# Computing the softmax bias of 256 attention blocks on ScalarE in place of GpSimd

## The chip, the cores and the metric

The program runs on one core of one Trainium2 chip. The metric is the device time of one execution in microseconds. Five engines work beside each other, each through its own queue in order: PE (TensorE), DVE (VectorE), ACT (ScalarE), POOL (GpSimd) and SP (SyncE, which here only issues DMAs).

## The reference

Two independent layers are computed and laid side by side in one output of 2048 rows and 2048 columns: attention with a sliding window, and a Fourier mixing layer written as matrix products.

```python
# A: S = 2048, D = 1024, 32 heads of 32, window W = 256
qkv = (x @ wqkv) ...                       # q, k, v
scores = jnp.einsum("bhqd,bhkd->bhqk", q, k) * (Dh ** -0.5)
mask = (idx[:, None] - idx[None, :] >= 0) & (idx[:, None] - idx[None, :] < W)
scores = jnp.where(mask[None, None], scores, -1e9)
o = jnp.einsum("bhqk,bhkd->bhqd", softmax(scores), v)
a = o.reshape(B, S, D) @ wo
# B
a_ = x @ dft_hid_re.T ;  b_ = x @ dft_hid_im.T
b = dft_seq_re @ a_ - dft_seq_im @ b_
out = concatenate([a, b], axis=-1)
```

## The kernel before

**Number format.** Every large product is made of fp16 matmuls: each operand is scaled by a power of two and split into a high part (ACT: a scaled copy to fp16) and a low part (DVE: the same value minus the high part), and three passes, high by high, high by low and low by high, are summed in PSUM (L720).

**Seven products in place of eight.** Most products run by `seven()`: of two by two blocks of each operand, sums are formed first and seven block products are made of them. Between two of these seven, ACT copies a PSUM bank into another (L1193), ACT or DVE evict finished banks (L1509, L1512, L1281, L1284, L431), and PE goes on in the next bank. There are four such banks, `m0` to `m3`.

**Stages.** First q, k and v of the attention are computed (up to some 600 us). Then the Fourier layer runs as a list of units: four rounds, each of eight "x" units (the product along the hidden dimension; results are split and summed into `tsum`, tile name `reg`, L432/L436/L1075) and eight "c" units (the product along the sequence; each loads two tiles of 128 rows of `in_cs`, looks at their largest value on ACT, L1001, scales and splits them on ACT and DVE, L1101 and L1102, and forms four sums on POOL, L1075). A place at which the x units of a round end and its c units begin is called a **turn** below; there are four. Last comes the product with `wo`.

**Attention runs inside these stages.** 256 blocks (8 groups of heads, 4 chunks of 512 rows, 2 pairs of heads, 4 blocks of 128 rows) are fed in between the large products by a counter of matmuls. One block is, in order: scores of two heads (PE, L586), the oldest key block folded in under the mask (DVE, L597), the negative largest score of each row (DVE, `mx`, L602), the softmax **bias** (L606 or L609), two exponentials, one for each head (ACT, L612), the high part (ACT, `hl`, L432), the low part (DVE, L436), one transposing DMA (SP, L621), two masks for the parts outside the window (POOL, `z` L627 and `t` L630). The product with v (PE, L662) follows four blocks later (`LAG`).

The step in question takes a tile of 128 x 2, multiplies it by a scale held per partition and adds a constant:

```python
            if BIAS == "ACT":
                op("ACT", 0.387, lambda: nc.scalar.activation(bias.t, mx.t, AF.Identity, bias=pshift, scale=es),
                   r=[mx, "pshift", ("esc", g // 2)], w=[bias])
            else:
                op("POOL", 0.28, lambda: nc.gpsimd.tensor_scalar(bias.t, mx.t, es, PSHIFT, op0=ALU.mult, op1=ALU.add),
                   r=[mx, ("esc", g // 2)], w=[bias], port=True)
```

**What sets the order.** The operations are not written in the order in which they run. `op()` records each with its engine, a cost in microseconds and what it reads and writes; `Plan.close` works a due time back from the matmuls; `Plan.run` then plays the program through with these costs and gives each free engine the ready operation that is due first. The resulting order is fixed in the program for all engines: a queue never overtakes. So a change of one operation's engine or cost can move any instruction after it. `port=True` marks operations of DVE and POOL that the plan keeps from running at the same time.

Of the kernel before, what the change touches and what calls it, by code (L numbers as in the profile page):

```python
# [46 lines left out]
STP = 4  # L47
RAWS = 6
TBUF = 6
BIAS = "POOL"  # L50
SUMS = ("POOL", "POOL", "POOL", "POOL")
XSUM = "DVE"
PLAIN = 3
# [46 lines left out]
class Plan:  # L100
# [4 lines left out]
    def op(self, eng, cost, fn, r=(), w=(), dma=None, port=False, loose=False):  # L105
        o = Op()
        o.eng, o.cost, o.fn, o.dma, o.port, o.loose = eng, cost, fn, dma, port, loose
        o.pre, o.suc, o.first, o.n, o.aim = set(), [], [], len(self.ops), None
        for k in (*r, *w):
            b = k[0] if isinstance(k, tuple) else k  # L110
            if isinstance(b, Buf) and (not b.ops or b.ops[-1] is not o):
                b.ops.append(o)
        for k in r:
            s = self.state.setdefault(k, [[], []])
            o.pre.update(s[0])
            s[1].append(o)
        for k in w:
            s = self.state.setdefault(k, [[], []])
            o.pre.update(s[0])
            o.pre.update(s[1])  # L120
            self.state[k] = [[o], []]
        o.pre.discard(o)
        self.ops.append(o)
        return o
# [209 lines left out]
def fused_kernel(ctx: ExitStack, tc: tile.TileContext, xa, wqk, wv, wo, xb, wd, cs, out):  # L334
# [194 lines left out]
    def attention():  # L529
# [33 lines left out]
        def s_step(b):  # L563
# [40 lines left out]
            es = escs[:, g // 2, sc:sc + 1]  # L604
            if BIAS == "ACT":
                op("ACT", 0.387, lambda: nc.scalar.activation(bias.t, mx.t, AF.Identity, bias=pshift, scale=es),  # L606
# [1088 lines left out]
```

## Time and profile before

| what | value |
|---|---|
| median of 3 runs | 1726.13 us (1724.79 to 1728.37) |
| the profiled execution | 1728.84 us |
| its span, first to last instruction | 1727.1 us |
| mean granted TensorE clock | 0.998 of full speed |
| DMA queue of SP | 363 MB, 81.6% of 16 engines' span |

The page of the profile lists busy times and the costliest groups of instructions; a group's line names the source line, the engine, the operation, output and inputs, its count, then busy time and mean duration, and after the second bar how long the engine stood idle just before and what ended that. The timeline lists single instructions with start and length, and the idle time of the engine before it in brackets. The windows list the busy time of each engine in a stretch of time.

### The profile page before, as it was taken

How to read it: one execution, taken by the hardware profiler on the slowest of the kernel's cores; microseconds unless marked ns; L12 is line 12 of the kernel's file. 1: busy time of each engine (PE TensorE's matmuls, PEld its weight loads, DVE VectorE, ACT ScalarE, POOL GpSimd, SP SyncE). 2: the span in 40 equal slices, each digit the busy share in tenths (PEclk: the TensorE clock that was granted, in tenths of full speed). 3: DMA queues.
4: the chain of work that ended last, by engine and by line, in shares of the span. 5: the costliest groups of instructions: out<-in, count | busy, mean ns of one | idle time of the engine just before them, and what ended most of it. 6: DMA issues, size and time to landing. Idle time of an engine off the chain costs nothing.

```text
span 1727.1 us, 31901 instructions
## 1 busy us (share of the span) xinstructions
PE 1690.3 (98%) x11607; PEld 908.6 (53%) x11607; DVE 1358.8 (79%) x2294; ACT 1051.5 (61%) x1678; POOL 771.6 (45%) x979
## 2 busy tenths in 40 slices
PE   8999999999999999999999999999999999999998
PEld 3446687675555445555544555545555545544443
DVE  6978997677988888777897986899985679879641
ACT  7555635456757788776675665776665576543322
POOL 0133501224535565635755755676664667611000
PEclk9999999999999999999999999999999999999999
DMA  6388799999998789998599998779999669983331
GB/s 266 121 329 326 229 309 272 267 244 244 221 278 204 159 200 246 215 273 194 98 233 274 246 278 175 151 153 255 238 261 224 141 129 207 215 264 110 110 98 74
DMA packets 469918, 368.36 MB, mean 213 GB/s; under 512 B 341760, under 2 KB 412416, under 8 KB 469760
## 3 DMA queue, kind: packets, MB, share of 16 engines
q1 hardware_dynamic: 468896, 363.17, 81.6%
q0 software_dynamic: 864, 3.15, 1.2%
q8 instruction: 91, 1.49, 0.4%
q14 instruction: 67, 0.55, 0.1%
HBM read 195.97 MB, written 96.86 MB: 170 GB/s over the span
## 4 chain that ended last, share of the span: by engine, by line
PE 83%; DVE 6%; ACT 4%; DMA 3%; issue 3%; POOL 1%; SPq 0%; POOLq 0%; DVEq 0%; ACTq 0%
PE m L720 74%; PE pv L662 4%; PE s L586 3%; PE old L586 1%; DVE st L1102 1%; DMA raw<-in_cs_dram 1%; DVE reg L439 1%; ACT junk L1001 1%; PE m L1323 1%; ACT s L612 1%; ACT reg L432 0%; DVE top L457 0%; DVE mx L602 0%; DVE s L597 0%; DMA late<-in_wo_dram 0%
## 5 line engine op out<-in xcount | busy, mean ns | idle before, releaser
L720 PE MATMUL m<-reg,st 128*128 128x512 f16 x4776 | 1101.1, 379 | 17.5 <-DVE st L1102 3.8
L720 PEld LDWEIGHTS <-st 128*128 128x128 f16 x5400 | 512.4, 98 | 579.1 <-issue 22.0
L612 ACT ACTIVATE s<-s,bias,escs 128x256 f32<-128x256 f32 (+1 forms) x512 | 270.5, 529 | 225.3 <-POOL bias L609 216.3
L609 POOL TENSOR_SCALAR bias<-mx,escs 128x2 f32<-128x2 f32 x256 | 114.2, 446 | 392.2 <-DVE mx L602 334.8
L1075 POOL TENSOR_TENSOR raw<-raw,raw 128x512 f32<-128x512 f32 x128 | 177.4, 1386 | 202.2 <-DVE st L1102 179.8
L436 DVE TENSOR_TENSOR hl<-s,hl 128x512 f16<-128x512 f32 (+1 forms) x256 | 170.6, 668 | 67.6 <-ACT hl L432 64.9
L627 POOL TENSOR_SCALAR_AFFINE_SELECT z<-t 128x512 f16<-128x512 f16 x224 | 174.2, 782 | 53.8 <-DMA t<-hl 41.3
L602 DVE TENSOR_REDUCE mx<-s 128x2 f32<-128x512 f32 (+1 forms) x256 | 170.8, 668 | 4.9
L630 POOL TENSOR_SCALAR_AFFINE_SELECT t<-t 128x512 f16<-128x512 f16 x224 | 169.5, 765 | 9.9
L432 ACT ACTIVATE hl<-s 128x512 f16<-128x512 f32 (+1 forms) x256 | 147.8, 578 | 8.2 <-DMA t<-hl 5.0
L720 PEld LDWEIGHTS <-reg 128*128 128x128 f16 x1212 | 116.3, 98 | 67.2 <-issue 5.2
L1101 ACT ACTIVATE st<-raw,sc 128x1024 f16<-128x1024 f32 x96 | 109.6, 1145 | 59.4 <-PE m L720 30.0
L1102 DVE SCALAR_TENSOR_TENSOR st<-raw,sc,st 128x1024 f16<-128x1024 f32 x96 | 135.8, 1418 | 11.9 <-ACT st L1101 10.7
L586 PEld LDWEIGHTS <-qk 96*128 96x128 f16 x1056 | 93.9, 98 | 81.5 <-issue 8.3
L597 DVE COPY_PREDICATED s<-upper,old 128x256 f32<-128x256 uint32 x224 | 94.6, 422 | 46.6 <-PE old L586 27.2
L720 PE MATMUL m<-reg 128*128 128x512 f16 x480 | 116.3, 382 | 3.5 <-ACT ybig L1509 3.0
L1512 DVE SCALAR_TENSOR_TENSOR ybig<-m,fu,ybig 128x512 f32<-128x512 f32 x112 | 83.4, 745 | 25.4 <-PE m L720 20.9
L720 PE MATMUL m<-xz,st 128*128 128x512 f16 x432 | 97.3, 379 | 2.7 <-ACT m L1193 2.5
L662 PE MATMUL pv<-vt,t 128*128 128x65 f16 x1984 | 98.3, 185 | 0.2
L586 PE MATMUL s<-qk,qk 96*128 96x128 f16 (+1 forms) x608 | 96.1, 253 | 2.0 <-DVE hl L436 1.5
L662 PEld LDWEIGHTS <-t 128*128 128x128 f16 x1984 | 88.3, 96 | 10.8 <-POOL t L630 0.4
L1001 ACT ACTIVATE junk<-raw 128x1024 uint8<-128x1024 f32 x82 | 86.3, 1052 | 10.2 <-DMA raw<-in_cs_dram 9.9
(172 smaller groups left out, 2130.9 us busy)
## 6 DMA issues: line engine op xcount, KB each, us to landing
raw<-in_cs_dram SPq DMA_DIRECT2D x64, 512.0 KB, 5.7
qk<-qs SPq DMA_DIRECT2D x192, 128.0 KB, 3.8
out_dram<-ybig SPq DMA_DIRECT2D x44, 512.0 KB, 4.9
qs<-ybig SPq DMA_DIRECT2D x64, 256.0 KB, 4.5
raw<-in_xb_dram SPq DMA_DIRECT2D x32, 512.0 KB, 5.3
raw<-in_wd_dram SPq DMA_DIRECT2D x32, 512.0 KB, 5.9
ybig<-out_dram SPq DMA_DIRECT2D x32, 512.0 KB, 4.9
vs<-ybig SPq DMA_DIRECT2D x32, 260.0 KB, 4.7
```

What stands on the lines that cost most here:

```text
L432: else nc.scalar.activation(dst(), src(), AF.Copy), r=r, w=w)
L436: op("DVE", c_dve(n), lambda: nc.vector.tensor_tensor(dst(), src(), hi(), op=ALU.subtract), r=r, w=w, port=port)
L586: nc.tensor.matmul(dst(j, a, e), qu.t[:, h, i * P:i * P + P], ku.t[:, h, ka:ke], start=True, stop=True, skip_group_check=True)
L602: dve(c_dve(2 * w), lambda: nc.vector.tensor_reduce(mx.t, sv(), axis=AX.X, op=ALU.max, negate=True), r=[(S, 0), (S, 1)], w=[mx])
L609: op("POOL", 0.28, lambda: nc.gpsimd.tensor_scalar(bias.t, mx.t, es, PSHIFT, op0=ALU.mult, op1=ALU.add), r=[mx, ("esc", g // 2)], w=[bias] ...
L612: op("ACT", 0.32 + 0.00085 * w, lambda h=h: nc.scalar.activation(sv()[:, h], sv()[:, h], AF.Exp, bias=bias.t[:, h:h + 1], scale=es), r=[bi ...
L627: op("POOL", 0.637, lambda: nc.gpsimd.affine_select(out=z.t, in_=pk(), compare_op=ALU.is_gt, fill=0.0, base=0, pattern=[[0, 4], [-1, P]], ...
L630: op("POOL", 0.637, lambda: nc.gpsimd.affine_select(out=pk(), in_=pk(), compare_op=ALU.is_ge, fill=0.0, base=0, pattern=[[0, 4], [1, P]], ...
L662: nc.tensor.matmul(pvt()[:, r, j, lo:], lhs, vt.t[:, k % QB, at + lo:at + VW], start=a, stop=e, skip_group_check=True)
L720: nc.tensor.matmul(ps.t[:, j * n:j * n + n], lhs(), rhs(), start=first, stop=last, skip_group_check=True)
L1075: lambda: e.tensor_tensor(o(), a(), b(), op=ALU.subtract if sub else ALU.add), r=r, w=w, port=True)
L1102: op("DVE", c_dve(n, True), lambda: nc.vector.scalar_tensor_tensor(dst(1), src(), scl(), dst(0), op0=ALU.mult, op1=ALU.subtract), r=[*r, s ...
```

## The change

One constant that chooses the branch above is set to the other value:

```diff
-BIAS = "POOL"
+BIAS = "ACT"
```

The 256 instructions at L609 on POOL go; 256 instructions at L606 on ACT come: an activation with the function Identity, a scale and a bias held per partition. The plan's cost of the step goes from 0.28 to 0.387 us, and the step is no longer marked as using the port that DVE and POOL share. From the first attention block on, the plan sorts the program anew. Of the 256 new instructions, 155 have the first exponential of their block straight behind them.

Early attention blocks on ACT: `s` is the tile of scores, `hl` the split exponentials, `m` a PSUM bank, `kf` a scale.

```order
 L431 ACTIVATE ybig<-m_16_2532,vf 128x16x32
+L606 ACTIVATE bias_3006<-mx_2998,pshift,escs 128x2
 L612 ACTIVATE s_2977<-s_2977,bias_3006,escs 128x256 x2
 L1281 ACTIVATE reg_81<-m_17_2848 128x512
 L432 ACTIVATE hl_3038<-s_2977 128x512
-L612 ACTIVATE s_3020<-s_3020,bias_3041,escs 128x256 x2
+L606 ACTIVATE bias_3042<-mx_3031,pshift,escs 128x2
+L612 ACTIVATE s_3020<-s_3020,bias_3042,escs 128x256 x2
 L431 ACTIVATE ybig<-reg_81,kf 128x512
```

The bias stands in front of its exponentials; the copies and evictions of `m` that follow stand behind both.

The first turn on POOL, before: the four sums (L1075) of one pair of `in_cs` tiles, `raw`, and the biases of three blocks.

```order
L609 TENSOR_SCALAR bias_7175<-mx_7168,escs 128x2
L1075 TENSOR_TENSOR raw_6931<-raw_6931,raw_5477 128x512
L1075 TENSOR_TENSOR raw_5477<-raw_5477 128x512
L609 TENSOR_SCALAR bias_7300<-mx_7271,escs 128x2
L1075 TENSOR_TENSOR raw_5477<-raw_5477,raw_6931 128x512
L609 TENSOR_SCALAR bias_7319<-mx_7311,escs 128x2
```

On ACT, before, the exponentials that need `bias_7300` stand in front of the bank copy L1193:

```order
L1101 ACTIVATE reg_81<-raw_5477,sc_7181 128x512
L612 ACTIVATE s_7195<-s_7195,bias_7300,escs 128x256 x2
L1193 ACTIVATE m_30_7316<-m_36_7260 128x512
L432 ACTIVATE hl_7321<-s_7195 128x512
L1101 ACTIVATE st_7329<-raw_5477,sc_7181 128x1024
```

After the change POOL's four sums stand together, and on ACT the same bank copy (`m_30`) stands behind the split `st_7289` of a summed `raw` and in front of the next bias:

```order
L612 ACTIVATE s_7175<-s_7175,bias_7250,escs 128x256 x2
L432 ACTIVATE hl_7280<-s_7175 128x512
L1101 ACTIVATE st_7286<-raw_6148,sc_7248 128x1024
L1101 ACTIVATE st_7289<-raw_5314,sc_7169 128x1024
L1193 ACTIVATE m_30_7299<-m_36_7234 128x512
L1101 ACTIVATE reg_81<-raw_6318,sc_7248 128x512
L1101 ACTIVATE st_7309<-raw_6923,sc_7169 128x1024
L606 ACTIVATE bias_7320<-mx_7294,pshift,escs 128x2
```

So the copy no longer stands behind exponentials that wait for POOL's bias, but behind a split that waits for POOL's sums.

The fourth turn on SP's queue, before: two `in_cs` loads, and six loads of q and k for the attention (`qk`).

```order
L621 DMA_TRANSPOSE t_18026<-hl_18011 128x8x128
L417 DMA raw_18041<-in_cs_dram 128x1024
L417 DMA qk_39_18050<-qs 32x4x512 x3
L417 DMA qk_31_18063<-qs 32x4x512 x2
L417 DMA raw_18072<-in_cs_dram 128x1024
L417 DMA qk_31_18063<-qs 32x4x512
```

and after:

```order
L621 DMA_TRANSPOSE t_17963<-hl_17911 128x8x128
L417 DMA raw_18011<-in_cs_dram 128x1024
L417 DMA raw_18027<-in_cs_dram 128x1024
L621 DMA_TRANSPOSE t_18039<-hl_18020 128x8x128
L417 DMA qk_39_18054<-qs 32x4x512 x3
L417 DMA qk_31_18066<-qs 32x4x512 x3
```

The second of the two loads stood behind five loads of q and k; now it stands straight behind the first.

The same turn on ACT, before: the looks (L1001, `junk`) at these two tiles and the evictions (L1509) of three banks. The look at the other tile of the pair, `raw_18041`, comes further down.

```order
L1001 ACTIVATE junk,top_18133<-raw_18072 128x1024
L1509 ACTIVATE ybig<-m_65_18081,fu_17758 128x512
L612 ACTIVATE s_18030<-s_18030,bias_18140,escs 128x256 x2
L1509 ACTIVATE ybig<-m_64_18076,fu_17758 128x512
L432 ACTIVATE hl_18167<-s_18030 128x512
```

and after:

```order
L1001 ACTIVATE junk,top_18098<-raw_18011 128x1024
L606 ACTIVATE bias_18113<-mx_18094,pshift,escs 128x2
L1001 ACTIVATE junk,top_18098<-raw_18027 128x1024
L612 ACTIVATE s_18043<-s_18043,bias_18113,escs 128x256 x2
L432 ACTIVATE hl_18132<-s_18043 128x512
L1509 ACTIVATE ybig<-m_64_18079,fu_17760 128x512
L1509 ACTIVATE ybig<-m_83_18048,fu_17760 128x512
```

Both looks now stand ahead of the evictions, and the eviction of bank `m_64` is the first of them. From the `wo` loads near the end on, SP's queue holds the same rows in the same order before and after.

## The prediction

> **What bounds the kernel now.** I read the page first: busy times, then the groups that the change touches.
>
> ```profile
> PE 1690.3 (98%) x11607; PEld 908.6 (53%) x11607; DVE 1358.8 (79%) x2294; ACT 1051.5 (61%) x1678; POOL 771.6 (45%) x979
> ...
> L612 ACT ACTIVATE s<-s,bias,escs 128x256 f32<-128x256 f32 (+1 forms) x512 | 270.5, 529 | 225.3 <-POOL bias L609 216.3
> L609 POOL TENSOR_SCALAR bias<-mx,escs 128x2 f32<-128x2 f32 x256 | 114.2, 446 | 392.2 <-DVE mx L602 334.8
> ```
>
> PE is busy 1690.3 of 1727.1 us. The matmuls stay the same, so whatever the other engines gain, the change can win no more than the missing 36.8 us and what a lowered clock costs; it loses what it adds to them. ACT's 216.3 us of waiting for the bias look large, but they cost only where PE then waits. So the windows come next, cut where PE is not full (columns: stretch, its length, busy PE, PEld, DVE, ACT, POOL, then the granted clock):
>
> ```profile
> 0.00:264.00 264.00, 255.09 (x1549) 154.42 (x1550) 223.43 (x288) 149.07 (x197) 62.71 (x70) 1.00 0.75 262
> 264.00:590.00 326.00, 325.94 (x2491) 191.80 (x2490) 256.23 (x454) 204.31 (x350) 134.56 (x202) 1.00 0.97 239
> 590.00:620.00 30.00, 25.39 (x189) 12.55 (x188) 27.12 (x65) 24.81 (x45) 12.97 (x16) 1.00 0.78 172
> 855.00:955.00 100.00, 94.65 (x649) 47.42 (x648) 87.49 (x154) 67.38 (x106) 59.52 (x66) 1.00 1.00 243
> 1125.00:1165.00 40.00, 36.32 (x227) 17.77 (x226) 37.23 (x59) 31.52 (x52) 28.30 (x31) 1.00 0.69 151
> 1415.00:1430.00 15.00, 11.78 (x56) 5.46 (x54) 10.04 (x24) 11.99 (x22) 6.33 (x8) 0.89 0.42 103
> 1530.00:1575.00 45.00, 39.51 (x174) 17.20 (x173) 40.59 (x45) 22.90 (x25) 7.52 (x4) 0.96 0.58 198
> 1575.00:1727.00 152.00, 147.28 (x682) 66.50 (x680) 74.35 (x83) 42.02 (x55) 0.00 (x0) 1.00 0.32 97
> ```
>
> Before 264 us there is no attention (PE lacks 8.9 us), and after 1530 hardly any of it is left (5.5 and 4.7 us). From 264 to 590 PE lacks 0.06 us although 256 blocks' chains have begun to run: there the bias costs nothing. What the change can touch is the four turns, at 590, 855, 1125 and 1415: 4.6 + 5.4 + 3.7 + 3.2 = **16.9 us**. That is the ceiling of the gain, with the clock lost at the fourth.
>
> **What goes and what comes.** POOL loses 256 instructions, 114.2 us (shortest, median and longest in ns, then the first and last start):
>
> ```profile
> L609 POOL TENSOR_SCALAR bias<-mx,escs x256: 262/266/1741, 263.7 to 1492.1; 128x2 f32<-128x2 f32 x128
> ```
>
> ACT gains 256 whose duration the trace doesn't show. Rows near it:
>
> ```profile
> L612 ACT ACTIVATE s<-s,bias,escs 128x256 f32<-128x256 f32 x480 | 256.8, 536 | 211.5 <-POOL bias L609 203.1
> ...
> L431 ACT ACTIVATE st<-raw,vB 128x1024 f16<-128x1024 f32 x16 | 18.3, 1146 | 2.6 <-PE m L720 2.4
> ...
> L432 ACT ACTIVATE st<-late 128x1024 f16<-128x1024 f32 x16 | 16.7, 1051 | 10.7 <-PE m L720 7.6 <-DVE late L1075 3.1
> ...
> L612 ACT ACTIVATE s<-s,bias,escs 128x128 f32<-128x128 f32 x32 | 13.7, 429 | 13.7 <-POOL bias L609 13.2
> ```
>
> The two exponentials give (536 - 429) / 128 = 0.84 ns an element, so 429 - 107 = 322 ns for almost none, with scale and bias per partition. The copies of SBUF give 1051 - 0.84 x 1024 = 191 ns, and 95 ns for each operand per partition (1146 - 1051): 0.38 us with two. I take 0.38, since the bias goes from SBUF to SBUF; the ends are 0.19 (no charge for the operands) and 0.43 (as the small exponential).
>
> How it queues, from the fourth turn on ACT:
>
> ```profile
> 1417.21 0.67 ACT L1509 ACTIVATE ybig<-m,fu 128x512 f32<-128x512 f32 x1
> 1417.78 1.10 ACT L612 ACTIVATE s<-s,bias,escs 128x256 f32<-128x256 f32 x2
> 1418.81 0.68 ACT L1509 ACTIVATE ybig<-m,fu 128x512 f32<-128x512 f32 x1
> ```
>
> Neighbours overlap by 0.10 us (1417.21 + 0.67 against 1417.78), while the pair, where the second waits for the first, takes 1.10 for two of 0.536: a gap of 0.03. So a bias with its exponential straight behind it delays ACT by 0.38 + 0.03, some 0.42 us, and one with other work between by 0.38 - 0.10 = 0.28. By the order there are 155 and 101: 65 + 28 = **93 us on ACT** (45 to 106 by the ends), 1051 to about 1145, 66% of the span. It is hidden wherever PE is full; it counts at turns where ACT is full.
>
> *First turn, +2.1 us.* ACT is busy 24.81 of 30 us there, and 4.24 of the rest is one wait that ends at 616.48 (below): up to 612 it is all but full. 22 us at 4.8 us a block (256 blocks over the 1230 us in which the bias instructions run, 264 to 1492) hold 4.6 blocks, at 0.28 each 1.3 us, if all of it reaches PE (ends 0 and 1.9). Then, on POOL, ACT and PE:
>
> ```profile
> 613.03 1.70 POOL L1075 TENSOR_TENSOR raw<-raw,raw 128x512 f32<-128x512 f32 x1 [4.21 <-DVE st L1102]
> 614.81 1.27 POOL L1075 TENSOR_TENSOR raw<-raw 128x512 f32<-128x512 f32 x1
> 616.18 0.27 POOL L609 TENSOR_SCALAR bias<-mx,escs 128x2 f32<-128x2 f32 x1
> 616.52 1.26 POOL L1075 TENSOR_TENSOR raw<-raw,raw 128x512 f32<-128x512 f32 x1
> ```
> ```profile
> 616.48 1.11 ACT L612 ACTIVATE s<-s,bias,escs 128x256 f32<-128x256 f32 x2 [4.24 <-POOL bias L609]
> ```
> ```profile
> 618.12 1.02 PE L720 MATMUL m<-reg,st 128*128 128x512 f16 x4 [0.37 <-ACT m L1193]
> ```
>
> The bias stood behind two POOL sums, which had waited for DVE, ACT behind the bias for 4.24 us, and PE lost 0.37. That wait goes, but what is late next is in the new order: the bank copy L1193 stands behind a split that needs the third sum. Three sums from 613.03 (1.70, 1.27 and 1.26, no bias between) end at 617.3, the split takes 1.1, so the copy starts near 618.4 and not at 617.5: 0.8 us more, not 0.37 less.
>
> *Third turn, -1.0 us.* On ACT, then PE:
>
> ```profile
> 1132.38 1.11 ACT L612 ACTIVATE s<-s,bias,escs 128x256 f32<-128x256 f32 x2 [0.95 <-POOL bias L609]
> ```
> ```profile
> 1136.67 2.75 PE L720 MATMUL m<-reg,st 128*128 128x512 f16 x12 [1.07 <-ACT m L1193]
> ```
>
> ACT paused no more between the two (the timeline's next rows follow each other closely), so 0.95 of PE's 1.07 us hung on POOL's bias. The ends are 0, if ACT waits as long for the maximum itself, and -1.07.
>
> *Fourth turn, -4.2 us.* SP's queue, then ACT and PE:
>
> ```profile
> 1404.17 1.86 SPq L417 DMA_DIRECT2D raw<-in_cs_dram  x1
> 1406.13 2.29 SPq L417 DMA_DIRECT2D qk<-qs  x5
> 1408.51 0.38 SPq L417 DMA_DIRECT2D raw<-in_cs_dram  x1
> ```
> ```profile
> 1416.16 1.06 ACT L1001 ACTIVATE junk<-raw 128x1024 uint8<-128x1024 f32 x1 [5.68 <-DMA raw<-in_cs_dram]
> ```
> ```profile
> 1419.54 2.40 PE L720 MATMUL m<-reg 128*128 128x512 f16 x8 [2.70 <-ACT ybig L1509]
> ```
>
> The second load stands behind five others, lands at 1416.1, ACT waits 5.68 us for it, and the evictions behind it stop PE for 2.70. In the new order it follows the first load directly: issued 2.4 us earlier, landed near 1413.8. The look (1.1), the pair (1.1), the high part (0.5) and the now first eviction (0.7) end at 1417.0, against 1419.5: 2.5 of the 2.70 us go. The clock is the rest:
>
> ```profile
> 80.00:90.00 10.00, 8.14 (x39) 3.61 (x37) 8.49 (x8) 3.76 (x6) 5.08 (x4) 1.00 0.94 303
> 1420.00:1430.00 10.00, 10.00 (x46) 4.64 (x45) 8.53 (x18) 8.18 (x15) 6.06 (x7) 0.83 0.31 79
> ```
>
> After the gap PE was granted 0.83 for 10 us, 1.7 us lost; around 80 us a stop of 1.86 us left it at 1.00. Without the long gap the 1.7 go too. The ends are 0 (the load comes as late as now) and -4.9 (3.2 + 1.7). The Trainium skill ("TensorE: Matmul & The Clock Gate", Part 1) has the clock halved only after an idle window of about 3.4 us, and free-running; by it a stop of 2.70 us would not do, the 1.7 us would have another cause and stay, and the sum would be -1.8. The trace shows the drop straight behind such a stop, so I go by the rows.
>
> *Second turn and the tail, 0.* At 855 PE waits for DVE, whose work is unchanged; after 1530 SP's queue holds the same rows.
>
> **Sum**: +2.1 - 1.0 - 4.2 = -3.1 us. The profiled execution took 1728.84 us, 1.7 of it around its span; it would take 1725.7. The median of the runs is 2.7 below it, so I give 1726.1 - 3.1 = **1723.0 us**.
>
> **Rivals.** *Slower: ACT inherits POOL's waits for the maximum.*
>
> ```profile
> POOL bias L609 <- DVE mx L602: 334.8, 144, 9.4
> ACT s L612 <- POOL bias L609: 216.3, 130, 4.9
> ```
>
> POOL waited 144 times for `mx`, up to 9.4 us; now ACT stands there, with evictions queued behind it that PE needs. At the fourth turn 5.68 us of waiting stopped PE for 2.70, so some 3.0 us are covered; it decides when an ACT wait in front of an L1193 or L1509 passes 3.0. One wait of 9.4 costs 6.4 and the clock 1.7: 1723.0 + 8.1 = 1731.1. Against it: ACT already stands behind the same maxima, through POOL, and its longest wait is 4.9.
>
> *No change: the stalls only move.* The whole order after 264 us is sorted anew by planned costs, and the gains above hang on two or three places. If each turn keeps its share, 16.9 us, the time stays at 1726.
>
> *Much faster: DVE is relieved.* PE waits for DVE at the second and third turn (busy 87.49 of 100 and 37.23 of 40 us).
>
> Most biases on POOL take 0.27 us, some up to 1.74, on average 0.446 (both rows above): 0.18 us of each is something in the way. If what is in the way is DVE, and DVE loses as much by POOL, then 100 and 40 us of these turns, 21 and 8 blocks, give back 29 x 0.18 = 5.2 us: 1723.0 - 5.2 = 1717.8. Against it: POOL's sums and masks, which stay, hold POOL far longer than 256 instructions of 0.27 us. The Trainium skill ("GPSIMD Engine Reference", Key points) says that the two engines share their way into SBUF and get in each other's way when DVE reads two inputs there; the spread from 0.26 to 1.74 agrees, but no row shows DVE's side of the bias.
>
> **How the numbers follow.** Chances: forecast 0.40; no change 0.27; slower, by ACT's wait 0.19; much faster 0.14. A measurement of this kernel can tell about 0.2% (3.5 us) from no change. The forecast lies just inside that, and what I am least sure of, the fourth turn, can take it past either edge; I count it 0.18 faster, 0.18 no change, 0.04 slower. Of no change, 0.07 may come out faster and 0.05 slower, since a new order scatters. Faster: 0.18 + 0.07 + 0.14 = 0.39. Slower: 0.04 + 0.05 + 0.19 = 0.28. No change: 0.33. The range runs from 1715.5, a little under the much faster case (its 5.2 us with the first turn's 2.1 not lost gives 1715.7), to the slower case at 1731.
>
> **What would show it.** L606 should have 256 instructions of 0.32 to 0.43 us; ACT near 1145 us busy, POOL near 657. ACT's waits should name DVE `mx` and add up to less than 216 us. At the fourth turn the second `in_cs` load should land at least 2 us before the evictions need it, the stop of 2.70 us be gone and the granted clock 1.00. At the first turn PE should lack more than 4.6 us, with ACT named, and the bank copy behind a split. The forecast is wrong if PE has a stop over 2 us that the profile puts down to an ACT instruction queued behind an L606, or if the second turn, where I expect nothing, moves by more than 2 us.

## The result and the profile after

| | median, us | lowest to highest | runs |
|---|---|---|---|
| before | 1727.25 | 1724.79 to 1729.90 | 6 |
| after | 1714.51 | 1713.18 to 1719.56 | 6 |

The ratio is 0.993, with a 95% interval of 0.9915 to 0.9946: 12.7 us faster (in a second batch 10.8: 1714.79 against 1725.62, ratio 0.9934). The ratios here and below come from all runs of a batch and need not be the quotient of the two medians. The forecast had the direction and a quarter of the size, and the time lies just below its range.

The profiled execution of the changed kernel took 1719.56 us, 5.05 above its median (span 1717.9). So a second profile of the same kernel is used beside it, with a span of 1710.7 us (1712.40 us, of runs with a median of 1714.79).

The page of after, busy times and the groups of the change:

```profile
PE 1689.5 (98%) x11607; PEld 909.1 (53%) x11607; DVE 1354.5 (79%) x2294; ACT 1135.5 (66%) x1934; POOL 663.0 (39%) x723
...
L612 ACT ACTIVATE s<-s,bias,escs 128x256 f32<-128x256 f32 (+1 forms) x512 | 270.7, 529 | 13.3
L606 ACT ACTIVATE bias<-mx,pshift,escs 128x2 f32<-128x2 f32 x256 | 98.2, 384 | 185.7 <-DVE mx L602 184.8
```

The bias takes 384 ns on ACT, as was estimated (0.38 us), and ACT waits 184.8 us for the maximum where it had waited 216.3 us for POOL's bias. The exponentials themselves now wait for almost nothing. ACT's list of waits gives the count and the longest:

```profile
ACT bias L606 <- DVE mx L602: 184.8, 128, 4.8
```

No wait is longer than 4.8 us. The windows of after (the columns are those of the prediction's windows):

```profile
264.00:590.00 326.00, 325.31 (x2513) 192.13 (x2511) 258.15 (x457) 228.30 (x420) 113.78 (x136) 1.00 0.98 241
590.00:620.00 30.00, 26.16 (x139) 12.34 (x138) 27.40 (x61) 28.64 (x53) 10.47 (x10) 0.96 0.77 180
...
855.00:960.00 105.00, 99.36 (x665) 49.57 (x664) 90.13 (x162) 74.86 (x128) 49.00 (x51) 0.98 0.99 233
1125.00:1165.00 40.00, 40.00 (x237) 20.13 (x236) 36.05 (x61) 35.41 (x63) 22.22 (x20) 1.00 0.66 149
...
1400.00:1430.00 30.00, 30.00 (x160) 14.71 (x159) 26.32 (x48) 25.73 (x47) 10.66 (x11) 1.00 0.71 155
...
1520.00:1566.00 46.00, 42.78 (x197) 19.02 (x195) 44.27 (x48) 25.19 (x27) 7.51 (x4) 1.00 0.60 210
```

At the third and the fourth turn PE is full: 40.00 of 40 and 30.00 of 30 us, where it had lacked 3.7 and 3.2 (0.5 us of idle time of the third lie behind its window, at 1168). The tail lacks 3.2 in place of 5.5. The table sums PE's idle time over the gaps of each stretch, from the traces; the cuts (580, 640, 840, 970, 1110, 1180, 1385, 1440, 1515 and 1580 us) lie where PE is nearly full in these kernels. The first four columns are the turns, the quiet stretches are what lies between the turns and the tail from 264 us on. PE's last gap (0.8 us) and the 4.0 us behind its last matmul are the same in every run; the latter are left out.

| PE idle, us | first | second | third | fourth | tail | quiet stretches | before 264, and PE's last gap | span |
|---|---|---|---|---|---|---|---|---|
| before | 4.6 | 5.4 | 3.7 | 3.4 | 5.5 | 0.5 | 9.8 | 1727.1 |
| after | 3.9 | 5.6 | 0.5 | 0.0 | 3.2 | 1.6 | 9.5 | 1717.9 |
| after, second profile | 3.8 | 4.4 | 0.0 | 0.0 | 2.7 | 1.3 | 10.0 | 1710.7 |

From before to the second profile PE's idle time falls by 10.6 us, and the clock gives back some 3.4 (15 x 0.11 at the fourth turn and 45 x 0.04 in the tail, from the prediction's windows; the second profile's clock is 1.00 throughout). That is 14 of 16.4 us of span; about 2 us are not assigned. The first profile of after is longer because of one stop. PE's timeline of it, and its windows:

```profile
913.41 0.19 PE L662 MATMUL pv<-vt,z 128*128 128x65 f16 x1 [3.09 <-DVE o L673]
```
```profile
913.40:923.40 10.00, 9.99 (x61) 4.66 (x62) 7.54 (x10) 3.89 (x5) 4.35 (x7) 0.83 1.13 219
```

DVE was held there behind a look at an `in_cs` tile that landed late. The stop of 3.09 us was followed by 10 us at a granted 0.83; in the second profile the same stop is 1.71 us and the clock stays at 1.00. At the first turn too, the first profile has 10 us at 0.83 and the second none. The 1.4 us of the stop and twice 1.7 of the clock are 4.8 of the 7.2 us between the two spans.

### The profile page after: what moved, and what is told of

It reads as the page before. It is cut to its first block, busy times and chain, and to the rows that moved or that the text cites. A ratio compares the mean times of both kernels' runs of the same rounds, so it can differ in the third digit from the quotient of the medians.

```text
span 1717.9 us, 31784 instructions
## 1 busy us (share of the span) xinstructions
PE 1689.5 (98%) x11607; PEld 909.1 (53%) x11607; DVE 1354.5 (79%) x2294; ACT 1135.5 (66%) x1934; POOL 663.0 (39%) x723
## 4 chain that ended last, share of the span: by engine, by line
PE 79%; DVE 8%; ACT 5%; DMA 4%; issue 3%; POOL 0%; SPq 0%; DVEq 0%; ACTq 0%; POOLq 0%
PE m L720 69%; PE pv L662 4%; PE s L586 3%; PE old L586 1%; DMA raw<-in_cs_dram 1%; ACT st L1101 1%; DVE reg L439 1%; ACT junk L1001 1%; DVE st L1102 1%; ACT s L612 1%; DMA t<-hl 1%; PE m L1323 1%; DVE top L457 1%; DVE late L1075 1%; DVE mx L602 1%
## 5 line engine op out<-in xcount | busy, mean ns | idle before, releaser
L1075 POOL TENSOR_TENSOR raw<-raw,raw 128x512 f32<-128x512 f32 x128 | 176.7, 1381 | 275.4 <-DVE st L1102 239.9
L606 ACT ACTIVATE bias<-mx,pshift,escs 128x2 f32<-128x2 f32 x256 | 98.2, 384 | 185.7 <-DVE mx L602 184.8
L720 PEld LDWEIGHTS <-reg 128*128 128x128 f16 x1212 | 115.9, 97 | 63.7 <-issue 1.8
L1102 DVE SCALAR_TENSOR_TENSOR st<-raw,sc,st 128x1024 f16<-128x1024 f32 x96 | 128.2, 1340 | 13.2 <-ACT st L1101 12.8
L1001 ACT ACTIVATE junk<-raw 128x1024 uint8<-128x1024 f32 x82 | 86.1, 1050 | 8.6 <-DMA raw<-in_cs_dram 8.4
```

Of the source, the lines that this page charges most:

```text
L720: nc.tensor.matmul(ps.t[:, j * n:j * n + n], lhs(), rhs(), start=first, stop=last, skip_group_check=True)
L1075: lambda: e.tensor_tensor(o(), a(), b(), op=ALU.subtract if sub else ALU.add), r=r, w=w, port=True)
L1102: op("DVE", c_dve(n, True), lambda: nc.vector.scalar_tensor_tensor(dst(1), src(), scl(), dst(0), op0=ALU.mult, op1=ALU.subtract), r=[*r, s ...
```

## The experiments

Theories are named by letters in what was expected. At first there were three. **Q**: the gain comes from the bias leaving POOL's queue, since ACT no longer waits behind POOL's sums and masks. **O**: it comes from the new order of the whole program, whichever engine computes the bias. **P**: POOL's 256 instructions fewer leave DVE undisturbed. Later came **M** (the plan had taken POOL's bias too cheap, 0.28 for a real 0.446 us), **G** (an order is good if the plan's cost is at least the real one), **E** (the engine sets a level) and **L** (each new order is a draw from a spread). All runs were timed beside the kernel before; its medians in these batches were 1725.6 to 1726.8 us.

### Order and engine apart

First the order of before with the instruction given to ACT; then the order of after with it given to POOL. The plan sees no difference.

```diff
 op("POOL", 0.28,
-   lambda: nc.gpsimd.tensor_scalar(bias.t, mx.t, es, PSHIFT, op0=ALU.mult, op1=ALU.add),
+   lambda: nc.scalar.activation(bias.t, mx.t, AF.Identity, bias=pshift, scale=es),
```

> The plan of before is kept word for word (bias planned on POOL at 0.28 us, so PE, DVE and SP run the old order), only the instruction is issued to ACT's queue at the place that the plan gives it. Theory Q (what counts is that exponentials and evictions on ACT no longer wait behind POOL's queue): most of the 12.7 us gain is here, 1713 to 1719. Theory O (what counts is the new order that the plan makes of the changed cost and engine): no gain, 1724 to 1730, perhaps slower, since ACT's new 98 us were not planned for.

```diff
 op("ACT", 0.387,
-   lambda: nc.scalar.activation(bias.t, mx.t, AF.Identity, bias=pshift, scale=es),
+   lambda: nc.gpsimd.tensor_scalar(bias.t, mx.t, es, PSHIFT, op0=ALU.mult, op1=ALU.add),
```

> The plan of after is kept word for word (bias planned on ACT at 0.387 us), only the instruction is issued to POOL's queue, as before. Theory Q: the gain is gone, 1724 to 1730 or more. Theory O: the gain stays, 1712 to 1718, since PE, DVE and SP run the order of after and ACT is spared 98 us.

| median, us | bias on POOL | bias on ACT |
|---|---|---|
| order of before | 1726.3 | 1736.51 (ratio 1.007 [1.0042, 1.0097]) |
| order of after | 1729.71 (1.0021 [1.0012, 1.003]) | 1714.51 |

Neither half gains anything alone. The old order with ACT loses 10 us, the new order with POOL 3; together they gain 12.7. So Q alone and O alone both fall. Where each part acts is read from the stretches:

| PE idle, us | first | second | third | fourth | tail | quiet stretches |
|---|---|---|---|---|---|---|
| old order, ACT | 5.8 | 7.6 | 4.0 | 5.4 | 4.6 | 3.5 |
| new order, POOL | 4.4 | 6.5 | 0.4 | 0.3 | 2.8 | 9.3 |

With the new order the third and fourth turns come clear on either engine (0.4 and 0.3, against 3.7 and 3.4 before), and the tail halves (2.8 against 5.5). With the old order the idle time stays (4.0, 5.4 and 4.6), although POOL is out of the way. The fourth turn on ACT and PE, in the old order with the bias on ACT:

```profile
1426.44 1.06 ACT L1001 ACTIVATE junk<-raw 128x1024 uint8<-128x1024 f32 x1 [5.40 <-DMA raw<-in_cs_dram]
```
```profile
1430.09 1.89 PE L720 MATMUL m<-reg 128*128 128x512 f16 x8 [2.70 <-ACT ybig L1509]
```

It is the wait of before (5.68 and 2.70 us there): the load stands behind the five others again.

What the new order loses with POOL it loses in the quiet stretches: 9.3 us against 1.6. Its windows:

```profile
264.00:590.00 326.00, 322.91 (x2476) 190.08 (x2473) 253.71 (x453) 203.72 (x350) 134.46 (x201) 1.00 0.98 239
...
1165.00:1400.00 235.00, 232.10 (x1783) 122.41 (x1781) 187.07 (x356) 143.60 (x240) 141.08 (x192) 1.00 0.92 214
...
1430.00:1525.00 95.00, 92.94 (x696) 47.72 (x694) 80.86 (x156) 54.30 (x85) 55.84 (x71) 1.00 0.99 222
```

One block shows how. The timelines of DVE, POOL, ACT and PE, new order with the bias on POOL:

```profile
1477.91 0.68 DVE L602 TENSOR_REDUCE mx<-s 128x2 f32<-128x512 f32 x1
```
```profile
1476.20 1.69 POOL L627 TENSOR_SCALAR_AFFINE_SELECT z<-t 128x512 f16<-128x512 f16 x1
1477.96 0.64 POOL L630 TENSOR_SCALAR_AFFINE_SELECT t<-t 128x512 f16<-128x512 f16 x1
1478.55 1.74 POOL L627 TENSOR_SCALAR_AFFINE_SELECT z<-t 128x512 f16<-128x512 f16 x1
1480.38 0.27 POOL L606 TENSOR_SCALAR bias<-mx,escs 128x2 f32<-128x2 f32 x1
```
```profile
1480.68 1.11 ACT L612 ACTIVATE s<-s,bias,escs 128x256 f32<-128x256 f32 x2 [2.60 <-POOL bias L606]
```
```profile
1483.19 0.38 PE L586 MATMUL s<-qk,qk 96*128 96x128 f16 x4 [0.96 <-DVE hl L436]
```

The maximum is done at 1478.59. The bias stands behind three masks, two of them of 1.7 us in place of 0.64, beside DVE's splits, and the last of them still runs when the maximum is there; the bias ends at 1480.65, the exponentials start 2.09 us after the maximum, and PE, which needs the tile of scores back, stops for 0.96 us. The same block in after, on DVE and ACT:

```profile
1469.01 0.68 DVE L602 TENSOR_REDUCE mx<-s 128x2 f32<-128x512 f32 x1
```
```profile
1469.73 0.39 ACT L606 ACTIVATE bias<-mx,pshift,escs 128x2 f32<-128x2 f32 x1 [0.81 <-DVE mx L602]
1470.15 1.11 ACT L612 ACTIVATE s<-s,bias,escs 128x256 f32<-128x256 f32 x2
```

Here the exponentials start 0.46 us after the maximum, and PE doesn't stop. The order is the same; the plan had counted 0.387 us for the bias, and on POOL it was there 2.06 us after the maximum.

### The instructions without the dependence

A second bias that nobody reads is computed on the other engine at the same place: in after on POOL, in before on ACT.

```diff
-op("ACT", 0.387, lambda: nc.scalar.activation(bias.t, ...),
+op("ACT", 0.387, lambda: (nc.scalar.activation(bias.t, ...),
+                          nc.gpsimd.tensor_scalar(spare_bias, mx.t, es, PSHIFT, ...)),
```

> After, with a second, unused bias computed on POOL at the same place in the order, so POOL has its 256 instructions, its waits for mx and its share of the port back, but nothing waits for their result. Theory P (POOL's time: sums and masks were late because POOL stood waiting for mx): the gain is gone, 1724 to 1730. Theory Q, in which only ACT's wait for POOL counts: 1713 to 1718. Theory O: 1713 to 1718.

> Before, with a second, unused bias computed on ACT at the same place in the order, so ACT has the 256 instructions of 0.38 us and the waits for mx of after, while the exponentials still wait for POOL. It prices ACT's load alone. My forecast's first turn (ACT full, +1.3 us): 1727 to 1731. If ACT's load is hidden everywhere: 1725 to 1728, as before. If evictions behind the waits stop PE: 1731 or more.

After with POOL's instructions back took 1718.67 us (ratio 0.9956 [0.9942, 0.9971]), 4.2 above after, whose interval (0.9915 to 0.9946) it just touches. Its group (the added line moves the numbers by one or two):

```profile
L608 POOL TENSOR_SCALAR spare_bias<-mx,escs 128x2 f32<-128x2 f32 x256 | 117.1, 458 | 385.3 <-DVE mx L603 325.7 <-DVE rs L669 29.6 <-DVE topone L465 9.8
```

POOL is as loaded as in the new order with POOL's bias (117.1 us against 115.9), only nobody waits for it. So in the new order the dependence on POOL costs 1729.71 - 1718.67 = 11.0 us and POOL's load some 4. The quiet stretches agree: summed as in the tables, PE lacks 2.2 us there, against 9.3 when the exponentials wait for POOL. P holds for a part. Its picture of DVE does not: with POOL's instructions back DVE is busy 1355.6 us, as in the two profiles of after (1354.5 and 1355.3); how POOL's load costs its 4 us was not shown. DVE's longest split (L1102), 1418 ns before, takes 1340 ns in after, and in the new order with the bias still on POOL it is as short:

```profile
L1102 DVE SCALAR_TENSOR_TENSOR st<-raw,sc,st 128x1024 f16<-128x1024 f32 x96 | 128.6, 1344 | 14.0 <-ACT st L1101 13.6
```

That shortening is the order's. Before with ACT's 256 instructions added took 1733.58 us (1.0047 [1.0029, 1.0065]): in the old order ACT's load, with its waits for `mx`, costs some 7 us. In its profile the first turn is as before (4.7 us idle in place of 4.6), and the quiet stretches lack 4.4 us in place of 0.5: the 93 us on ACT are not hidden wherever PE was full. What they cost in the new order, no run shows alone.

### What the plan believes

M says that an order made with POOL's true cost wins; the changed number is the plan's only (from before: 0.446 and 0.300 for 0.28; from after: 0.360 and 0.420 for 0.387).

```diff
-op("POOL", 0.28, ...
+op("POOL", 0.446, ...
```

> Before, with the plan's cost of the bias on POOL raised from 0.28 to the 0.446 us that the trace of before shows as its mean. Theory M (order and engine have to match: what hurts in before is that the plan takes POOL's bias for shorter than it is, so that ACT's and PE's order is wrong by the difference 256 times): a good part of the gain, 1714 to 1721. Theory L (orders scatter, the one of after is a lucky one): anywhere in 1720 to 1734. Theory E (POOL is a bad place for the step however it is planned): 1724 to 1730.

> Before, with the plan's cost of the bias on POOL changed from 0.28 to 0.30 us: an order of no special merit, to measure how far orders scatter. Theories M and E: within 3 us of before, 1723 to 1730. Theory L: 5 us and more away is as likely as not.

> After, with the plan's cost of the bias on ACT changed from 0.387 to 0.36 us, 0.024 under the 0.384 that it takes: another order for the same engines. Theories M and E: within 3 us of after, 1711 to 1718. Theory L: nearer to before, 1718 to 1730.

> After, with the plan's cost of the bias on ACT changed from 0.387 to 0.42 us, close to what a bias with its exponential straight behind it delays ACT: another order for the same engines. Theories M and E: 1711 to 1718. Theory L: 1718 to 1730.

With its true cost, POOL's version took 1730.18 us (1.0017 [1.0001, 1.0032]): M falls. With 0.300 it took 1724.30 (0.9982 [0.9971, 0.9994]), with ACT at 0.360 1726.20 (1.0001 [0.9986, 1.0016]), at 0.420 1714.73 (0.9927 [0.9906, 0.9948]). A change of 0.027 us in a number of the plan took back the whole gain. Since ACT's bias really takes 0.384, this left two readings, G and L:

> After, unchanged, for a second profile: the profiled execution of after took 1719.56 us, the median of its runs 1714.51. If the stop of 3.09 us that its trace shows at 910 us belongs to the program, it is there again; if it belongs to that execution, it is gone or under 1 us and the granted clock is higher. Median 1713 to 1716.

> After, planned cost of the bias on ACT 0.40 us. Theory G (a plan that gives ACT at least the 0.384 us which the bias takes is met by the chip; one that gives less is not, and ACT falls behind it): 1712 to 1719, as 0.387 and 0.42. Theory L (orders scatter whatever the cost): 1712 to 1730, as likely above 1719 as below.

> After, planned cost of the bias on ACT 0.45 us, 0.066 more than it takes. Theory G: 1712 to 1720. Theory L: 1712 to 1730, as likely above 1719 as below.

After came out at 1714.79 (0.9934 [0.9915, 0.9953]). Its stop at 910 us was there again, but of 1.71 us, which is neither of the two outcomes named. At 0.400 the time was 1723.15 (0.9982 [0.997, 0.9994]), so G falls. At 0.450 it was **1711.59** (0.9912 [0.9896, 0.9927]), the fastest version here, clearly ahead of before; from after, 1714.79 in the same batch, the intervals do not part it. Two of its windows:

```profile
590.00:620.00 30.00, 29.11 (x184) 14.73 (x183) 28.27 (x62) 26.94 (x52) 10.00 (x8) 1.00 0.59 159
...
1510.00:1560.00 50.00, 49.01 (x227) 21.99 (x226) 46.66 (x52) 25.00 (x27) 8.70 (x6) 1.00 0.57 202
```

It clears the first turn and the tail, which after does not (0.9 in place of 3.8 us, and 1.0 in place of 3.2).

### Engine or draw

More orders for each engine, and the bias on DVE, where it needs no other engine's queue (`dve(C_TINY, ...tensor_scalar...)` in place of the POOL line). With 0.35 us on POOL there is no order to time: the plan leaves operations unplaced.

> Before, planned cost of the bias on POOL 0.26 us: a fourth order with the bias on POOL. Theory E+L (orders scatter by several us around a level that the engine sets, near 1727 on POOL and near 1718 on ACT, as the three and five orders so far average): 1722 to 1732. Theory L alone (one scatter for both engines, 1711 to 1730): as likely under 1721 as over.

> Before, planned cost of the bias on POOL 0.32 us: a fifth order with the bias on POOL. Theory E+L: 1722 to 1732. Theory L alone: as likely under 1721 as over.

> After, planned cost of the bias on ACT 0.50 us. Theory G (the plan gives ACT slack of 0.1 us a block and the chip keeps to it): 1709 to 1716, like 0.45 (1711.6) and 0.42 (1714.7). Theory E+L: 1710 to 1726.

> The bias planned and run on DVE at 0.155 us, behind the reduction that gives mx, so neither POOL nor ACT holds it and no engine is crossed twice. Theory E+L with POOL's load as the reason (the unused bias on POOL beside after cost 4 us): near the ACT level, 1711 to 1722. If DVE, 79% busy and about 90% at the turns, can't take 256 more instructions of 0.15 us (39 us, 0.6 to 1.2 us at each of the four turns and a later release of everything behind them): 1722 to 1732.

> Before, planned cost of the bias on POOL 0.40 us: a sixth order with the bias on POOL. Theory E+L (levels near 1730 on POOL and near 1718 on ACT, each with a scatter of some 6 us): 1723 to 1739, above the mean of the ACT orders, 1718. It speaks against it under 1718.

> After, planned cost of the bias on ACT 0.33 us, 0.05 less than it takes: a seventh order with the bias on ACT. Theory E+L: 1711 to 1727, under the mean of the POOL orders, 1730. It speaks against it over 1730. Theory G, already hurt by 0.40 us (1723.2), would want it above 1722.

| bias on | plan's cost: median, us | mean | standard deviation |
|---|---|---|---|
| POOL | 0.26: 1738.86; 0.28: 1726.3; 0.30: 1724.30; 0.32: 1731.22; 0.40: 1723.28; 0.446: 1730.18 | 1729.0 | 5.8 |
| ACT | 0.33: 1722.18; 0.36: 1726.20; 0.387: 1714.51; 0.40: 1723.15; 0.42: 1714.73; 0.45: 1711.59; 0.50: 1717.56 | 1718.6 | 5.4 |
| DVE | 1750.55 (1.0123 [1.0096, 1.015]) | | |

The means differ by 10.5 us, with a standard error of 3.1 (5.8 and 5.4 over the roots of 6 and 7), while the single orders overlap: the worst of ACT (1726.2) is slower than the best two of POOL. E and L both stand, if with misses: 0.26 on POOL (1738.86) lies above the 1732 that was expected, and 0.50 on ACT (1717.56) above G's 1716. About 10 us belong to the engine, with an order planned for it, and each order comes out some 5 to 6 us to either side. The gain is the engine's 10.5, plus 4.1 by which the draw on ACT is better than average (1714.5 against 1718.6), less 2.7 by which that on POOL was (1726.3 against 1729.0); that share is luck. The plan also keeps the step apart from DVE on POOL (`port=True`) and not on ACT. No run changes this mark alone, but POOL's bias in an order without it, the new order on POOL, took 1729.71, at POOL's mean.

Where the engine's 10 us lie can be read from the profiles of these orders, by the stretches of the table (the tail up to 1600 us, and for after the mean of its two profiles). PE idles 36.0 us on average with POOL and 29.5 with ACT. The 6.5 between them are 1.5 at the first turn, 1.5 at the second, 0.6 and 1.0 at the third and fourth, 1.3 in the tail and 0.9 in the quiet stretches, less 0.3 ahead of 264 us. The clock, lowered for 3.4 us twice on average with POOL and once with ACT, makes another 1.7; of the 10.4 us between the mean spans some 2 are not assigned. So the quiet stretches, where one block was followed above, hold only a small part of POOL's level; the rest lies at the turns and in the tail.

DVE's version, tried in one order, shows that a short way to the bias is not all. The bias follows `mx` on the same engine, but DVE was the fullest engine beside PE (79%); the bias took 379 ns there on average (median 228), where the plan counted 155, which may have hurt this order. PE's windows of it lack far more than the 0.06 and 5.4 us of before:

```profile
264.00:590.00 326.00, 319.87 (x2455) 187.78 (x2453) 263.80 (x514) 200.87 (x345) 107.81 (x134) 1.00 0.94 237
...
840.00:970.00 130.00, 117.63 (x762) 58.15 (x761) 110.56 (x201) 81.31 (x128) 61.34 (x62) 0.99 0.85 193
```

## Why the prediction was right or wrong

**Costs: right.** 384 ns for each bias (0.38 taken), ACT 1135.5 us (1145), POOL 663.0 (657), ACT's waits for `mx` 184.8 us, under 216. The Trainium skill ("ScalarE: Activation LUTs", What ACT_TABLE_LOAD costs) gives 186 ns, 0.833 ns an element and 93 ns for each operand per partition; that makes 374 ns, and the measured 384 agrees.

**Fourth turn, -4.2: right in cause, and near in size.** PE's idle time went from 3.4 to 0.0 us and the clock from 0.89 to 1.00, some 5 us in all. The cause is the load order, as argued: the stop comes back with the old order whichever engine has the bias, and is gone with the new one. The clock's part was luck, as shown below. (Without it the prediction's sum would be -1.4 us, not the -1.8 that it names: 2.1 - 1.0 - 2.5.)

**Third turn, -1.0: the direction right, the cause wrong and the size too small.** It lost 3.2 to 3.7 us. The step said that PE's 1.07 us hung on POOL's bias. With the bias on ACT in the old order the turn still lacks 4.0; with it on POOL in the new order 0.4. The same place in the old order with the bias on ACT, on ACT and PE:

```profile
1142.09 0.39 ACT L609 ACTIVATE bias<-mx,pshift,escs 128x2 f32<-128x2 f32 x1 [1.36 <-DVE mx L602]
```
```profile
1147.69 2.75 PE L720 MATMUL m<-reg,st 128*128 128x512 f16 x12 [1.34 <-ACT m L1193]
```

ACT waits 1.36 us for the maximum itself, and PE still stops, for 1.34: this is the end of 0 that the prediction had named. So it was the order of the work around the turn. The term also rests on one of four gaps; the other three (0.37, 0.59 and 1.64) went as well.

**First turn, +2.1: wrong in sign.** ACT is as full there as forecast (28.64 of 30 us), but PE lacks 3.9 us and not 6.7. ACT's and PE's timelines of after:

```profile
614.95 2.18 ACT L1101 ACTIVATE st<-raw,sc 128x1024 f16<-128x1024 f32 x2
617.03 0.58 ACT L1193 ACTIVATE m<-m 128x512 f32<-128x512 f32 x1
```
```profile
616.68 0.38 PE L586 MATMUL s<-qk,qk 96*128 96x256 f16 x2 [1.19 <-DVE hl L436]
617.67 2.56 PE L720 MATMUL m<-reg,st 128*128 128x512 f16 x6 [0.61 <-ACT m L1193]
```

The bank copy does stand behind two splits, and PE waits 0.61 us for it in place of 0.37. But the splits had their sums in time, so it starts at 617.03 and not at the forecast 618.4. The forecast had kept the start of the sums from the old order, 613.03; in the new one POOL starts them 1.9 us earlier:

```profile
611.09 1.71 POOL L1075 TENSOR_TENSOR raw<-raw,raw 128x512 f32<-128x512 f32 x1 [6.70 <-DVE st L1102]
```

The 1.3 us of ACT's extra load don't show in PE's idle time: the other gaps of this turn sum to 3.2 us, where they had been 4.2. In the first profile the turn then lost 1.7 us of clock, so there it cost about 1 us more than before; in the second it did not.

**Tail, 0: wrong.** "After 1530 SP's queue holds the same rows" is true, but rows in the same order are not rows at the same time. SP's, ACT's and PE's timelines of after:

```profile
1518.34 4.99 SPq L417 DMA_DIRECT2D late<-in_wo_dram  x8
```
```profile
1524.37 1.15 ACT L431 ACTIVATE ext<-late,vwo 128x1024 f16<-128x1024 f32 x1 [0.98 <-DMA late<-in_wo_dram]
```
```profile
1522.04 2.75 PE L720 MATMUL m<-reg 128*128 128x512 f16 x12
...
1527.55 1.67 PE L720 MATMUL m<-reg,st 128*128 128x512 f16 x7 [0.17 <-DVE reg L1512]
```

and of before:

```profile
1525.81 5.41 SPq L417 DMA_DIRECT2D late<-in_wo_dram  x8
```
```profile
1532.37 1.15 ACT L431 ACTIVATE ext<-late,vwo 128x1024 f16<-128x1024 f32 x1 [3.63 <-DMA late<-in_wo_dram]
```
```profile
1527.39 2.75 PE L720 MATMUL m<-reg 128*128 128x512 f16 x12
...
1535.55 1.93 PE L720 MATMUL m<-reg,st 128*128 128x512 f16 x7 [2.82 <-DVE reg L1512]
```

The `wo` loads are issued 7.5 us earlier than before, the matmuls on PE run 5.35 us earlier (1522.04 against 1527.39). So the loads have gained 2.1 us on PE, and the one that ACT needs 2.65: ACT waits 0.98 for it and not 3.63, and PE, behind ACT and DVE, 0.17 and not 2.82. With the stop went the lowered clock behind it. The prediction's ceiling of 16.9 us, from the four turns, had left these 4.6 us out. The same 2.65 us can be followed through the three engines; no run moved these loads alone.

**Second turn, 0, and the quiet stretches, 0.** The second moved by +0.2 in one profile and -1.0 in the other, inside the 2 us that were named. The quiet stretches lost 1 us more than before. Both hold for the pair of kernels. They don't hold for the parts: with the new order and POOL's bias the quiet stretches lack 9.3 us. (Of the 256 biases 67 run between 264 and 590 us of before, not all, as the prediction has it.) That PE is full in a stretch of before says that this order covers POOL's bias there, not that any order does.

**The sum.** -3.1 was forecast against 12.7 measured. The step that failed is the same one in three places: outside of the rows that had been compared, the new order was taken as neutral (the tail was put at 0, the third turn at its one gap, the first at the old start of its sums), and it was not. They make 2.7 and 2.9 us (idle time of the third and first turn, second profile against forecast) and 2.8 + 1.8 (idle time and clock of the tail): 10.2 us, where 9.6 were missing. The two do not match exactly: the second profile lies 2.4 us below its median, and the profile of before 1.6 above.

**The rivals.** ACT's inherited waits stopped PE nowhere for long; the longest is 4.8 us, not 9.4, and between 264 and 1580 us PE's stops behind L1193 and L1509 sum to 2.1 us in place of 6.2. DVE's relief, the rival whose 1717.8 lies nearest to the result, is not what made the gain: its 0.18 us of each of 256 blocks would be 46 us of DVE, whose busy time fell by 4.3 (1358.8 to 1354.5), and L1102 is as short with POOL's bias in the new order. "The stalls only move" holds between orders: a different number in the plan gave 1726.2 on ACT.

**The clock.** The prediction let the clock drop behind a stop of 2.70 us. Behind the same length of stop, 2.70, the old order with ACT kept 1.00:

```profile
1430.00:1440.00 10.00, 9.55 (x48) 4.50 (x48) 8.71 (x20) 9.77 (x20) 5.57 (x5) 1.00 0.29 79
```

So such a stop may cost the 1.7 us or not. Nor must it be one stop: at the first turn of after three stops (0.39, 1.19 and 0.61 us) lie within 2.9 us, and the first profile then ran at

```profile
616.50:626.50 10.00, 9.21 (x37) 3.96 (x37) 7.55 (x10) 7.01 (x13) 8.71 (x8) 0.83 0.82 223
```

while the second, with the same three stops, stayed at 1.00.

The clock records of the 19 traces show what decides. Each drop goes to 0.50 and lasts 3.41 us (one lasts 6.83), which loses the 1.7 us and makes the 0.83 over 10 us. Within one execution the drops begin whole multiples of 3.41 us apart (in before at 1420.78 and 1536.83, 34 such steps); the drop behind the last matmul lies on the same steps. So time can be cut into steps, and what matters is how long PE idles in one of them. The steps around the three stops, in the first profile of after and in the second:

```profile
614.45:617.86 3.41, 1.22 (x7) 0.53 (x6) 3.38 (x8) 3.40 (x5) 3.26 (x4) 1.00 0.87 230
617.86:621.27 3.41, 3.41 (x9) 1.21 (x8) 3.41 (x4) 3.31 (x6) 2.19 (x2) 0.50 1.04 173
```
```profile
612.11:615.52 3.41, 2.33 (x16) 1.17 (x15) 3.27 (x13) 3.19 (x6) 3.17 (x4) 1.00 1.23 172
615.52:618.94 3.42, 2.32 (x11) 1.07 (x11) 3.42 (x5) 3.39 (x6) 3.06 (x3) 1.00 1.09 294
```

In the first the stops fall into one step, 2.2 us idle, and the next step runs at half the clock; in the second they are shared by two steps, 1.1 us each. So it is with the two stops of 2.70 us: before has 2.2 us of idle time in one step, the old order with ACT 1.35 and 1.88 in two. Over all traces, from 10 us to the last matmul, each of the 17 steps with 2.0 us of idle time or more was followed by a drop, of 35 steps with 1.5 to 2.0 us 6 were, and of those with less none but the second step of the long drop. The Trainium skill ("TensorE: Matmul & The Clock Gate", Part 1) names an idle window of about 3.4 us; the steps have that length, but PE was idle for only 1.5 to 3.0 us of those ahead of a drop, so here the measurement goes against it as a safe limit. Where the steps lie differs from execution to execution, so the 1.7 us of the fourth turn should have been a chance and not a certainty.

**What stays open.** The quiet stretches' loss by POOL was followed to a single block in one order only, and no block was followed at the turns, where the other orders for POOL lose most. Against 0.30, 0.26 idles 6.0 us more in the quiet stretches and 3.4 more at the fourth turn; why, was not traced. All orders come from one plan with one number changed, so the spread of 5 to 6 us is that of this family.

## What to carry to other kernels

Where a planner sorts the program, changing an operation's engine is two changes, the engine and a new order; run each alone (old order on the new engine, new order on the old engine) before crediting either, and draw several orders before trusting one, since here a cost moved by 0.013 us was worth 8.6 us. A small step between two engines should not go through a third engine's queue of long work, even if that engine is the least busy; raising the plan's cost to the step's mean duration there did not help (1730.18), and a cost that holds the wait in that queue was not tried. In a forecast, look at every gap of a stretch and compare the loads' time against the engine that needs them, not their order alone.

## What the runs showed of the hardware

- A TENSOR_SCALAR of 128 x 2 on POOL has a median of 266 ns and a longest of 1741; its masks of 128 x 512 have a median of 0.64 us, and two that ran beside DVE's splits took 1.69 and 1.74. The same bias on ACT stayed within 368 to 413 ns in both profiles of after.
- Two executions of the same program differ by 7.2 us of span; 3.1 of it came from one load that landed later, by way of a stop and the clock behind it.
- The granted clock falls to a half for 3.41 us, on steps of 3.41 us that are fixed within an execution. All 17 steps with 2.0 us or more of idle PE were followed by a drop, 6 of 35 with 1.5 to 2.0; a stop of 2.70 us that two steps share left the clock at 1.00.
